# The first gate and up pair as seven-product units, and a new handover from keys and values to the units

## The chip, the cores and the metric

The kernel runs on one core of one Trainium2 chip. The metric is the device time of one execution in microseconds (us). The engines of a core work side by side, each through its own list of instructions in order: TensorE (PE in the profile, its weight loads PEld), VectorE (DVE), ScalarE (ACT), GpSimd (POOL) and SyncE (SP). SP and POOL here only start DMAs, each into a queue of its own. They meet through semaphores: an instruction at the head of its list waits until what it reads is written and what it overwrites has been read, and everything behind it on that engine waits too.

## What is computed

Two branches share one input of 2048 tokens by 1024 and are mixed by a sigmoid gate for each token.

```python
g = _sigmoid((x * gate_w).sum(-1, keepdims=True))
a = _A_ref(x, A_wqkv, A_w_phi, A_wo)          # linear attention, 32 heads of 32
b = _B_ref(x, B_w_gate, B_w_up, B_w_down)     # gelu(x @ w_gate) * (x @ w_up) @ w_down, 3584 hidden
return g * a + (1 - g) * b

# in _A_ref, per head: q, k, v from x @ wqkv
pq, pk = q @ w_phi, k @ w_phi
phi_q = concat(softmax(pq), softmax(-pq));  phi_k = concat(softmax(pk), softmax(-pk))
kv = phi_k.T @ v;  z = phi_k.sum(over tokens)
o = (phi_q @ kv) / (phi_q @ z + 1e-6);  a = o @ wo
```

## The kernel before

**Numbers and passes.** All matrices are float32. A factor is kept as two float32r tiles, a high part (a copy by ACT: `high`, or the first half of `split`) and a low part (the rest, a subtraction by DVE: `low`). A product of two factors is three matmuls per 128 rows of depth: `PASSES` is high by high, high by low, low by high.

**First and second keys-and-values pass.** The tokens are four blocks of 512 (`BLK`). The loop `for hh in range(2)` makes keys and values of 16 heads for all tokens, in 16 chunks of 128 tokens. A chunk is 48 matmuls (`keys_values`, L202): 24 into a PSUM bank of keys (`m` = 0), 24 into a bank of values (`m` = 1). `features` turns the keys into both softmaxes: on DVE a maximum, a minimum and two subtractions (L209 to L213), ACT takes the exponential, and then come the split of the values (`vs`), a sum, a reciprocal, a product and the split into `f`; `accumulate` (L235, 8 matmuls) adds the chunk to `kv` two chunks later. Four PSUM banks (`turn_bank`) hold keys and values and four (`bank`) hold the running `kv`. `meanwhile` names what DVE does beside a chunk: the split of a part of x for a later block (`load_x`), or the gate's logits for 128 tokens (`gate`, one DVE instruction over 1024 columns). In the second pass the split x of blocks 0 and 1 is made a second time, since the first pass overwrote it, and `query_weights` folds `w_phi` into the query weights (L136), for eight head groups, one half of the fold after each half of a chunk. Loads come through `stage`, three buffers of 512 KB filled by SP.

**Units.** Gate, up and query projections run as units: one unit takes two blocks of 512 tokens (a half) and two blocks of 128 weight columns, and makes the four results by seven products in place of eight (a Strassen scheme). A product is 12 matmuls (`product`, L768). A unit has seven slots; its products `c` ("z", operand 6) and "v" (operand 5) run in slots 2 and 4 of the next unit. The products need sums of the x blocks (`x_sums`: four DVE instructions for each quarter of the depth; split into `xs`, operands 1, 2, 4, 5) and sums of the weight blocks (x, y, z and v in `weights`). PE and DVE follow program order, in the units ACT and SP do so too. The order of DVE and ACT work within the units comes from a planner (`run_slot`) which keeps a clock for DVE and ACT, and due times in slots for each piece.

**The handover.** The first pair of gate and up columns for the first half isn't made by units: `project` (L103) makes it plainly, eight times 24 matmuls, between the keys and values and the first unit. Under these 192 matmuls DVE and ACT make the x sums of the first half, the last features, the split of z and the first unit's weights. The first half has 30 units then, the second 32.

**The turn.** When the second half begins, `second_half` (L535 and on) loads its operands in 14 parts through four buffers. After part n is split, SP loads part n + 4 into the buffer just read (`load`, L551). `late_sums` makes the second half's x sums earlier, beside the units of the first.

After the units, the down and output projections (L1203) follow; the change doesn't touch them.

Of the kernel before, what the change touches and what calls it, by code (L numbers as in the profile page):

```python
# [16 lines left out]
P = 128  # L17
KC = D // P
# [13 lines left out]
def tile_gated_mix(ctx: ExitStack, tc: tile.TileContext, x, xT, wkT, wqT, wv, w_phi, wo,  # L32
# [56 lines left out]

    def new_weight():  # L90
        return ring.tile([P, 2, KC, P], F32R, tag="wgu", name="wgu", bufs=2)
# [32 lines left out]
    xs_late = [dram.tile([P, KC // 2, BLK], F32, name=f"xs{k}") for k in range(4)]  # L124
# [16 lines left out]

    PE, DVE, ACT, SP = (getattr(mybir.EngineType, n) for n in ("PE", "DVE", "Activation", "SP"))
    with tc.tile_pool(name="kw", bufs=1) as kw, tc.tile_pool(name="kp", bufs=1) as kp, \
            tc.tile_pool(name="kl", bufs=1) as kl, tc.manual_schedule(engines={PE, DVE}):
        ones = kp.tile([P, P], F32, name="ones")
        nc.vector.memset(ones, 1.0)
        mask = kp.tile([P, 4, 32], F32, name="mask")
        nc.vector.memset(mask, 0.0)
        for j in range(4):
            nc.vector.memset(mask[32 * j:32 * j + 32, j, :], 1.0)  # L150
        ones_r = kp.tile([P, P], F32R, name="ones_r")
        nc.vector.tensor_copy(ones_r, ones)
        phi_c = kp.tile([P, NG, 32], F32, name="phi_c")

        warm = turn_bank()
        for _ in range(7):
            nc.tensor.matmul(warm[:, :P], ones, ones, start=True, stop=True)
        nc.scalar.dma_start(phi_c, w_phi.rearrange("(g h) d f -> (h d) g f", h=4))

        spare = []  # L160
        for tag, n in (("vs", 1), ("f", 2)):
            for _ in range(2):
                t = kp.tile([P, n, 1024], F32, tag=tag, name="early", bufs=2)
                spare += [t[:, i] for i in range(n)]
        for _ in range(2):
            t = ring.tile([P, 2, 1024], F32, tag="wgu", name="early", bufs=2)
            spare += [t[:, i] for i in range(2)]
        spare = [kp.tile([P, 1024], F32, tag="gw", name="early", bufs=1)] + spare
        zb = kl.tile([P, NG, 2, 32], F32, name="zb")

        def gate(c):
            s = stage((0, 1024, x[c * P:(c + 1) * P, :]))
            nc.vector.scalar_tensor_tensor(s, s, 1.0, gw, op0=OP.mult, op1=OP.mult,
                                           accum_out=logit[:, c:c + 1])

        def block_diagonal(hh):
            bd = kw.tile([P, 4, 4, 32], F32, name="bd")
            for j in range(4):
                nc.vector.tensor_tensor(bd[:, j], phi_c[:, 4 * hh + j:4 * hh + j + 1, :].to_broadcast([P, 4, 32]),
                                        mask, OP.mult)  # L180
            return bd

        def staged_pair(hh, kc, into=None):
            return stage((0, 512, wkT[hh, kc]), (512, 512, wv[hh, kc]), into=into)

        def fold(hh, kc, bd, s=None, pf=None):

            s = staged_pair(hh, kc) if s is None else s
            w = kw.tile([P, 2, 1024], F32R, tag="wkv", name="wkv", bufs=KC)
            pf = bank() if pf is None else pf  # L190
            for j in range(4):
                nc.tensor.matmul(pf[:, j * P:(j + 1) * P], s[:, j * P:(j + 1) * P],  # L192
                                 bd[:, j].rearrange("p a b -> p (a b)"), start=True, stop=True)
            with urgent():
                split(w[:, 0, 512:], w[:, 1, 512:], s[:, 512:])
                split(w[:, 0, :512], w[:, 1, :512], pf)
            return w

        def keys_values(ps, w, b, t, kc, parts=range(2)):
            for i, (a, e) in enumerate(PASSES):  # L200
                for m in parts:
                    nc.tensor.matmul(ps[m], xb[b, kc // 4][:, a, kc % 4, t * P:(t + 1) * P], w[:, e, m * 512:(m + 1) * 512],  # L202
                                     start=kc == 0 and i == 0, stop=kc == KC - 1 and i == 2)

        def features(ps, vs, f, zacc, first):

            pk = ps[0].rearrange("p (h f) -> p h f", f=32)
            mm = kp.tile([P, 2, 16], F32, tag="mm", name="mm", bufs=2)
            nc.vector.tensor_reduce(mm[:, 0, :], pk, AX.X, OP.max)  # L209
            nc.vector.tensor_reduce(mm[:, 1, :], pk, AX.X, OP.min)  # L210
            e = kp.tile([P, 2, 16, 32], F32, tag="e", name="e", bufs=2)
            nc.vector.tensor_tensor(e[:, 0], pk, mm[:, 0, :].unsqueeze(2).to_broadcast([P, 16, 32]), OP.subtract)
            nc.vector.tensor_tensor(e[:, 1], mm[:, 1, :].unsqueeze(2).to_broadcast([P, 16, 32]), pk, OP.subtract)  # L213
            nc.scalar.activation(e, e, AF.Exp)
            yield
            split(vs[:, :, 0], vs[:, :, 1], ps[1].rearrange("p (a b) -> p a b", b=64))
            yield
            r = kp.tile([P, 2, 16], F32, tag="r", name="r", bufs=2)
            nc.vector.tensor_reduce(r, e, AX.X, OP.add)
            nc.vector.reciprocal(r, r)  # L220
            yield
            nc.vector.tensor_tensor(e, e, r.unsqueeze(3).to_broadcast([P, 2, 16, 32]), OP.mult)
            yield
            split(f[:, 0], f[:, 1], e.rearrange("p s h f -> p s (h f)"))
            yield
            if first:
                nc.vector.tensor_copy(zacc, e)
            else:
                nc.vector.tensor_tensor(zacc, zacc, e, OP.add)

        def accumulate(pkv, vs, f, first, last):

            for d in range(8):
                heads = slice(64 * d, 64 * d + 64)
                nc.tensor.matmul(pkv[d // 2][:, d % 2], vs[:, d].rearrange("p a b -> p (a b)"), f[:, :, :, heads],  # L235
                                 start=first and d % 2 == 0, stop=last, skip_group_check=True)

        def finish_kv(hh, pkv):

            t = kp.tile([P, 4, 2, 2, 64], F32, tag="e", name="kv_t", bufs=2)  # L240
            for n, p in enumerate(pkv):
                nc.scalar.activation(t[:, n], p[:, :, 0], AF.Copy)
                nc.vector.tensor_tensor(t[:, n], p[:, :, 1], t[:, n], OP.add)
            low_rows = kp.tile([P, 4, 2, 2, 64], F32, tag="e", name="kv_l", bufs=2)
            nc.scalar.activation(low_rows[:64], t[64:], AF.Copy)
            nc.vector.tensor_tensor(t[:64], t[:64], low_rows[:64], OP.add)
            kv_c = kl.tile([P, 4, 2, 2, 32], F32, name="kv_c")
            for h in range(2):
                q = slice(32 * h, 32 * h + 32)
                nc.vector.transpose(kv_c[q].rearrange("p a b c d -> p (a b c) d"),  # L250
                                    t[q].rearrange("p a b c d -> p (a b c) d")[:, :, q])
            for s in range(2):
                nc.gpsimd.dma_start(kz[0][64 * s:64 * s + 64, 4 * hh:4 * hh + 4], kv_c[:64, :, :, s])

        def z_parts(zacc, zs):
            zs = zs.rearrange("p i (s a) b -> p i s (a b)", s=2)
            split(zs[:, 0], zs[:, 1], zacc.rearrange("p s h f -> p s (h f)"))
            return zs

        def finish_z(hh, zs, parts=range(2)):  # L260
            for s in parts:
                pz = bank() if hh else turn_bank()
                for i in range(2):
                    nc.tensor.matmul(pz, ones_r, zs[:, i, s], start=i == 0, stop=i == 1)
                z4 = pz.rearrange("p (g h f) -> p g h f", g=4, h=4)
                for h in range(4):
                    q = slice(64 * s + 32 * (h % 2), 64 * s + 32 * (h % 2) + 32)
                    nc.scalar.activation(zb[q, 4 * hh:4 * hh + 4, h // 2], z4[q, :, h, :], AF.Copy)

        gates = list(range(S // P))  # L270

        def meanwhile(hh, n, chunks):

            x_part = lambda b, j: lambda: load_x(b, (j,))
            done, part = divmod(n - 3, 4)
            if hh == 0 and n < 3:
                return [x_part(1, j) for j in ((0,), (1, 2), (3,))[n]]
            if done in (0, 1):
                return [x_part((chunks[4 * done][0] + 2) % 4, part)]
# [965 lines left out]
```

## Time and profile before

| | us |
|---|---|
| median of 3 runs (2365.52 to 2365.89) | 2365.73 |
| the profiled execution: its own time | 2365.71 |
| the profiled execution: span from first to last instruction | 2363.9 |
| PE busy | 2357.4 |
| DVE busy | 1800.6 |
| ACT busy | 1054.1 |

The span is 1.8 us shorter than the time of the same execution; this difference lies around the program. By the timeline the two keys-and-values passes end at 414.6 us from the start, the plain projections at 461.0, the units at 1674.1, and the rest is the two last projections. Spans of matmuls are modelled, so the distance from one matmul's start to the next one's tells more than the busy time: 12 matmuls of 512 columns take 2.72 us.

### The profile page before, as it was taken

To read this page: it belongs to the slowest core of one execution; us is meant where nothing else is said; L and a number is where in the kernel's file an instruction comes from. 1 tells how busy PE (TensorE), PEld (TensorE's weight loads), DVE (VectorE), ACT (ScalarE), POOL (GpSimd) and SP (SyncE) were. 2 spreads that over 40 slices of the span, in tenths; PEclk is the share of its full clock that TensorE was granted. 3 is DMA by queue.
4 is the path that set the end of the run, shared out by engine and by line. 5 is a ranking of instruction groups with operands and counts; after the bars stand their busy time and mean duration, and the time that the engine had idled before them with its cause. 6 is when DMAs were issued, how large, how long until landed. Compare 5 with 4: busy or idle time off the path is not lost.

```text
span 2363.9 us, 28280 instructions
## 1 busy us (share of the span) xinstructions
PE 2357.4 (100%) x10625; PEld 1958.3 (83%) x10625; DVE 1800.6 (76%) x2353; ACT 1054.1 (45%) x1380; POOL 159.2 (7%) x297
## 2 busy tenths in 40 slices
PE   9999999999999999999999999999999999999999
PEld 8888888888888888888888888888888888888887
DVE  7887878878798777767888877777574868867873
ACT  4324332546545544456565666665433323323221
POOL 0000000111111111110010000000000000000000
PEclk9999999999999999999999999999999999999999
DMA  5112233544454556474444444444784767977874
GB/s 177 49 45 89 83 117 116 198 165 167 152 181 168 185 195 209 175 268 140 143 153 144 149 140 149 139 139 134 242 304 159 275 228 246 339 267 274 286 268 137
DMA packets 152618, 425.11 MB, mean 180 GB/s; under 512 B 21408, under 2 KB 21408, under 8 KB 152480
## 3 DMA queue, kind: packets, MB, share of 16 engines
q1 hardware_dynamic: 123840, 329.30, 42.0%
q0 software_dynamic: 27600, 93.87, 10.4%
q8 instruction: 83, 1.36, 0.2%
q14 instruction: 55, 0.45, 0.1%
q10 hardware_dynamic: 1040, 0.13, 0.0%
HBM read 328.34 MB, written 94.90 MB: 179 GB/s over the span
## 4 chain that ended last, share of the span: by engine, by line
PE 99%; DMA 1%; DVE 0%; issue 0%; ACT 0%; SPq 0%; DVEq 0%
PE po L1203 29%; PE a L768 21%; PE pd L202 15%; PE c L768 14%; PE b L768 7%; PE p L768 7%; PE pg L235 1%; PE misc L980 1%; PE pd L103 1%; PE pg L103 1%; PE pd L136 1%; PE pd L192 0%; DMA early<-in_wkT 0%; DMA stage<-in_w_gate 0%; PE pg L192 0%; DMA phi_c<-in_w_phi 0%
## 5 line engine op out<-in xcount | busy, mean ns | idle before, releaser
L202 PE MATMUL pd<-wkv,x 128*128 128x512 f32 x1536 | 360.0, 391 | 0.0
L202 PEld LDWEIGHTS pd<-wkv,x 128*128 128x128 f32 x1536 | 284.8, 188 | 57.3 <-DVE x L44 0.3
L1203 PE MATMUL po<-tw,wgu 128*128 128x512 f32 x1344 | 309.8, 389 | 0.0
L1203 PEld LDWEIGHTS po<-tw,wgu 128*128 128x128 f32 x1344 | 252.3, 188 | 52.3
L414 ACT ACTIVATE wgu<-stage 128x1024 fp32r<-128x1024 f32 x147 | 155.4, 1057 | 236.6 <-DVE stage L1093 160.6
L417 DVE TENSOR_TENSOR wgu<-stage,wgu 128x1024 fp32r<-128x1024 f32 x147 | 179.2, 1219 | 78.8 <-ACT wgu L414 77.8
L417 DVE TENSOR_TENSOR tyz<-stage,tyz 128x1024 fp32r<-128x1024 f32 x126 | 153.4, 1217 | 51.7 <-ACT tyz L414 51.7
L768 PE MATMUL b<-s,tyz 128*128 128x512 f32 x744 | 179.0, 389 | 1.1 <-DVE s L417 1.1
L768 PE MATMUL a<-s,tyz 128*128 128x512 f32 x744 | 179.1, 389 | 0.0
L768 PE MATMUL p<-s,tyz 128*128 128x512 f32 x744 | 178.9, 389 | 0.0
L768 PE MATMUL a<-s,v 128*128 128x512 f32 x744 | 178.8, 389 | 0.0
L768 PE MATMUL c<-x,tyz 128*128 128x512 f32 x744 | 178.8, 389 | 0.0
L768 PE MATMUL c<-x,wgu 128*128 128x512 f32 x744 | 178.8, 389 | 0.0
L768 PE MATMUL a<-x,wgu 128*128 128x512 f32 x744 | 178.7, 389 | 0.0
L768 PEld LDWEIGHTS b<-s,tyz 128*128 128x128 f32 x744 | 139.6, 188 | 30.5 <-DVE s L417 1.6
L768 PEld LDWEIGHTS a<-s,tyz 128*128 128x128 f32 x744 | 139.5, 188 | 29.5 <-DVE tyz L417 0.4
L768 PEld LDWEIGHTS c<-x,tyz 128*128 128x128 f32 x744 | 139.7, 188 | 29.3
L768 PEld LDWEIGHTS c<-x,wgu 128*128 128x128 f32 x744 | 139.7, 188 | 29.2
L768 PEld LDWEIGHTS p<-s,tyz 128*128 128x128 f32 x744 | 139.6, 188 | 29.0
L768 PEld LDWEIGHTS a<-s,v 128*128 128x128 f32 x744 | 139.6, 188 | 29.0
L768 PEld LDWEIGHTS a<-x,wgu 128*128 128x128 f32 x744 | 139.6, 188 | 29.0
L1203 PE MATMUL po<-tw,wl 128*128 128x512 f32 x672 | 157.2, 389 | 0.0
(186 smaller groups left out, 3506.7 us busy)
## 6 DMA issues: line engine op xcount, KB each, us to landing
stage<-lm SPq DMA_DIRECT2D x98, 512.0 KB, 4.7
sr<-in_w_down SPq DMA_DIRECT2D x84, 512.0 KB, 5.4
sl<-lm SPq DMA_DIRECT2D x70, 512.0 KB, 4.6
lm<-h POOLq DMA_DIRECT2D x112, 256.0 KB, 2.3
stage<-in_w_gate SPq DMA_DIRECT2D x43, 512.0 KB, 3.8
stage<-in_w_up SPq DMA_DIRECT2D x43, 512.0 KB, 3.7
stage<-la SPq DMA_DIRECT2D x28, 512.0 KB, 5.4
tg<-stage POOLq DMA_DIRECT2D x26, 512.0 KB, 3.0
```

Source lines behind the costliest of these rows:

```text
L103: nc.tensor.matmul(pg, w[:, a, kc, :], xb[b, kc // 4][:, e, kc % 4, :], start=kc == 0 and i == 0, stop=kc == KC - 1 and i == 2)
L136: nc.tensor.matmul(pf[:, j * P:(j + 1) * P], s[:, (4 * k + j) * P:(4 * k + j + 1) * P], bp.rearrange("p a b -> p (a b)"), start=True, stop ...
L202: nc.tensor.matmul(ps[m], xb[b, kc // 4][:, a, kc % 4, t * P:(t + 1) * P], w[:, e, m * 512:(m + 1) * 512], start=kc == 0 and i == 0, stop= ...
L235: nc.tensor.matmul(pkv[d // 2][:, d % 2], vs[:, d].rearrange("p a b -> p (a b)"), f[:, :, :, heads], start=first and d % 2 == 0, stop=last ...
L414: nc.scalar.activation(dst, src, AF.Copy)
L417: nc.vector.tensor_tensor(dst, src, dst_h.bitcast(F32), OP.subtract)
L768: nc.tensor.matmul(dst, w[:, h, 4 * part + kc, :], xq[:, e, kc, :], start=first and kc == 0 and i == 0, stop=kc == 3 and i == 2, skip_grou ...
L980: nc.tensor.matmul(po[p], kbs[:, p].rearrange("p a b -> p (a b)"), pts[:, q, p, :], start=q == 0, stop=q == 1)
L1203: nc.tensor.matmul(ps[c], lefts[s][:, a, m, c * P:(c + 1) * P], made[k][:, e, m], start=d == 0 and m == 0 and n == 0, stop=d == n_duo - 1 ...
```

## The change

The first half gets all 32 units: the first gate and up pair goes through units too, and the 192 plain matmuls go. So the x sums of the first half, the first unit's weights and the second unit's raw weights must be ready when the keys and values end.

- **First pass.** `store_x` writes the split x of blocks 0 and 1 to DRAM (`x_parts`, four DMAs of 2 MB on SP, at chunks 3, 5, 7 and 9). Eight of the gate's logits move here, one at each of chunks 3 to 10, beside the x part.
- **Second pass.** `reload_x` reads the split x back (four DMAs of 2 MB on SP) in place of eight loads and splits. `early_sums` makes the x sums of the first half (chunks 4, 5, 7, 8) and POOL writes them to DRAM (`x_sum`). Both halves of a query fold follow the chunk; four groups are folded there (chunks 1 to 4), the other four in the handover. The first unit's weights are made at chunks 9 and 11; the z sum of the first heads moves from chunk 1 to chunk 6.
- **`features`** adds to `zacc` before the low part of `f`, not after it. The split of the values stands by itself (`split_values`).
- **Chunks 14 and 15** of the second pass are woven: keys of 14, keys of 15, values of 14, values of 15.
- **Handover.** Between the last values and the first unit PE has four folds and two `accumulate`; ACT and DVE follow an order written by hand. The pools are closed and opened so that new tiles may wait for single tiles (`reuse_waits="tile"`).
- **Turn.** `second_half` loads part n + 3 after part n, into the buffer that part n - 1 has left.

```diff
+    def store_x(b, k):
+        nc.sync.dma_start(x_parts[b][k], xb[b, k].bitcast(F32))
+    def reload_x(b, k):
+        xb[b, k] = new_quarter(b, k)
+        nc.sync.dma_start(xb[b, k].bitcast(F32), x_parts[b][k])
...
+    def quarter_sums(e, o):
+        nc.vector.tensor_tensor(o[:, BLK:], o[:, BLK:], o[:, :BLK], OP.subtract)
+        nc.vector.tensor_tensor(o[:, :BLK], e[:, :BLK], o[:, :BLK], OP.subtract)
...
+        es = e.rearrange("p s h f -> p s (h f)")
+        nc.scalar.activation(f[:, 0], es, AF.Copy)
         if first:
             nc.vector.tensor_copy(zacc, e)
         else:
             nc.vector.tensor_tensor(zacc, zacc, e, OP.add)
+        yield
+        nc.vector.tensor_tensor(f[:, 1], es, f[:, 0].bitcast(F32), OP.subtract)
...
+    def early_sums(kc):
+        r1, r2 = (stage() for _ in range(2))
+        x_load(0, kc, r1, r2)
+        x_sums(0, kc, r1, r2)
...
+            if hh == 0:
+                works.append(x_part(done + 2, part))
+                if part % 2 == 0:
+                    store_x(done, part // 2)
+            elif part % 2 == 0:
+                reload_x(done, part // 2)
+        if n in GATES[hh]:
+            works.append(lambda c=gates.pop(0): gate(c))
+        if hh and n in SUMS:
+            works += [lambda: None] * (not works) + [lambda: early_sums(SUMS.index(n))]
+    SUMS = (4, 5, 7, 8)
+    GATES = (range(3, 14), (1, 2, 3, 6, 10))
...
+            elif hh and n == 14:
+                ps, later = ([turn_bank(), turn_bank()] for _ in range(2))
+                for kc in range(KC):
+                    keys_values(ps, wkv[kc], b, t, kc, (0,))
+                pending.pop(0)()
+                for kc in range(KC):
+                    keys_values(later, wkv[kc], *chunks[15], kc, (0,))
+                for kc in range(KC):
+                    keys_values(ps, wkv[kc], b, t, kc, (1,))
+                pending.pop(0)()
+            elif hh and n == 15:
+                ps = later
+                for kc in range(KC):
+                    keys_values(ps, wkv[kc], b, t, kc, (1,))
...
-        first_g = {0: project(first_w[0], 0, turn_bank())}
...
-        gs = [project(second_w, j) for j in range(2)]
...
+        folds = [fold_in(last_q[0], turn_bank)]
+        zs = slot().rearrange("p i (s a) b -> p i s (a b)", s=2)
+        split_values(ps, vs)
+        rest(folds[0])
+        for accumulate_last in pending:
+            accumulate_last()
+        folds.append(fold_in(last_q[1], turn_bank))
+        for i in range(2):
+            for do in early[i]: do()
+        raw_sum(2)
+        kv = finish_kv(1, pkv)
+        next(kv)
+        rest(folds[1])
+        high(zs[:, 0], z_rows)
+        rest(kv)
+        folds.append(fold_in(last_q[2], turn_bank))
+        rest(folds[2])
+        first_z = slot()
+        high(flat(first_z)[0], even_w)
+        low(flat(first_z)[1], even_w, flat(first_z)[0])
+        folds.append(fold_in(last_q[3], bank))
+        rest(folds[3])
+        for i in range(2, 4):
+            for do in early[i]: do()
+        raw_sum(3)
+        low(zs[:, 1], z_rows, zs[:, 0])
...
-                if n + 4 < len(parts):
-                    load(n + 4)
+                if 0 < n < len(parts) - 3:
+                    load(n + 3)
...
-            mine = [(half, k, m) for m in range(1 - half, NF // 2) for k in "gu"]
+            mine = [(half, k, m) for m in range(NF // 2) for k in "gu"]
...
+        late, early = (psum_b.enter_context(tc.tile_pool(name=n, bufs=1, space=PSUM, reuse_waits="tile"))
+                       for n in ("pl", "pe"))
...
+        clock[:] = 5.5, 4.2
```

`fold_in` issues the two halves of a fold (16 matmul instructions, into two banks); `fold_out`, run by `rest`, copies both banks by ACT and stores them by POOL. `early[i]` is the high and the low part of one half of `xs[0]` (i = 0, 1) or of `xs[1]` (i = 2, 3). The last line sets the planner's start clocks of DVE and ACT for the first unit.

More of the change, by code (lines that the diff above doesn't have):

```diff
@@ new lines, in tile_gated_mix @@
+    for _ in range(7):
+        nc.tensor.matmul(warm[:, :P], ones, ones, start=True, stop=True)
+    nc.scalar.dma_start(phi_c, w_phi.rearrange("(g h) d f -> (h d) g f", h=4))
+    spare = []
+    for tag, n in (("vs", 1), ("f", 2)):
+        for _ in range(2):
+            t = kp.tile([P, n, 1024], F32, tag=tag, name="early", bufs=2)
+            spare += [t[:, i] for i in range(n)]
+    for _ in range(2):
+        t = ring.tile([P, 2, 1024], F32, tag="wgu", name="early", bufs=2)
+        spare += [t[:, i] for i in range(2)]
@@ new lines, in staged_pair, with fold @@
+    def staged_pair(hh, kc, into=None):
+        return stage((0, 512, wkT[hh, kc]), (512, 512, wv[hh, kc]), into=into)
+    def fold(hh, kc, bd, s=None, pf=None):
+        s = staged_pair(hh, kc) if s is None else s
+        w = kw.tile([P, 2, 1024], F32R, tag="wkv", name="wkv", bufs=KC)
+        pf = bank() if pf is None else pf
+        for j in range(4):
+            nc.tensor.matmul(pf[:, j * P:(j + 1) * P], s[:, j * P:(j + 1) * P],
+                             bd[:, j].rearrange("p a b -> p (a b)"), start=True, stop=True)
+        with urgent():
+            split(w[:, 0, 512:], w[:, 1, 512:], s[:, 512:])
+            split(w[:, 0, :512], w[:, 1, :512], pf)
+        return w
@@ new lines, in accumulate, with finish_kv @@
+    def accumulate(pkv, vs, f, first, last):
+        for d in range(8):
+            heads = slice(64 * d, 64 * d + 64)
+            nc.tensor.matmul(pkv[d // 2][:, d % 2], vs[:, d].rearrange("p a b -> p (a b)"), f[:, :, :, heads],
+                             start=first and d % 2 == 0, stop=last, skip_group_check=True)
+    def finish_kv(hh, pkv):
+        t = kp.tile([P, 4, 2, 2, 64], F32, tag="e", name="kv_t", bufs=2)
+        for n, p in enumerate(pkv):
+            nc.scalar.activation(t[:, n], p[:, :, 0], AF.Copy)
+            nc.vector.tensor_tensor(t[:, n], p[:, :, 1], t[:, n], OP.add)
+        yield
+        low_rows = kp.tile([P, 4, 2, 2, 64], F32, tag="e", name="kv_l", bufs=2)
+        nc.scalar.activation(low_rows[:64], t[64:], AF.Copy)
+        nc.vector.tensor_tensor(t[:64], t[:64], low_rows[:64], OP.add)
+        kv_c = kl.tile([P, 4, 2, 2, 32], F32, name="kv_c")
+        for h in range(2):
+            q = slice(32 * h, 32 * h + 32)
+            nc.vector.transpose(kv_c[q].rearrange("p a b c d -> p (a b c) d"),
+                                t[q].rearrange("p a b c d -> p (a b c) d")[:, :, q])
+        for s in range(2):
+            nc.gpsimd.dma_start(kz[0][64 * s:64 * s + 64, 4 * hh:4 * hh + 4], kv_c[:64, :, :, s])
@@ new lines, in tile_gated_mix @@
+                if turn:
+                    wkv = fresh
+                if len(pending) > 1:
+                    pending.pop(0)()
+                if hh and n == 0:
+                    zs = z_parts(zacc, new_weight())
+                if hh == 0 and n == 14:
+                    bd = block_diagonal(1)
+            if n == 0:
+                zacc = kp.tile([P, 2, 16, 32], F32, name="zacc")
+                pkv = []
+            vs = kp.tile([P, 8, 2, 64], F32R, tag="vs", name="vs", bufs=2)
@@ new lines, in tile_gated_mix @@
+            f = kp.tile([P, 2, 2, 512], F32R, tag="f", name="f", bufs=2)
+            steps = features(ps, f, zacc, n == 0)
+            next(steps)
+            works = meanwhile(hh, n, chunks)
+            for work in works[:1]:
+                work()
+            if hh and n == 15:
+                split_values(*waiting)
+            if hh and n == 14:
+                waiting = ps, vs
+            elif not (hh and n == 15):
+                split_values(ps, vs)
+            if not (hh == 0 and n == 14):
+                for _ in steps:
+                    pass
@@ new lines, in tile_gated_mix, with values @@
+            for work in works[1:]:
+                work()
+            def values(hh=hh, pkv=pkv, vs=vs, f=f, n=n):
+                if n == 0:
+                    pkv += [bank((P, 2, 2, 2, 64)) for _ in range(4)]
+                accumulate(pkv, vs, f, n == 0, n == 15)
+                if n == 15 and hh == 0:
+                    for _ in finish_kv(hh, pkv):
+                        pass
+            pending.append(values)
+            if hh and n == 9:
+                odd_w, even_w = stage((0, 1024, wq_fold[1])), stage((0, 1024, wq_fold[0]))
+                first_x, first_y = new_weight(), new_weight()
+                pair = lambda w: [w[:, i].rearrange("p a b -> p (a b)") for i in range(2)]
+                split(*pair(first_x), even_w)
@@ L410, in slot @@
+    halves = ExitStack()
+    mid = ctx.enter_context(tc.tile_pool(name="mid", bufs=1, side="right", reuse_waits="tile"))
+    xa = halves.enter_context(tc.tile_pool(name="xa", bufs=1, side="right", reuse_waits="tile"))
+    homes = xa.tile([P, 2, 1024], F32, tag="pts", name="wq", bufs=1)
+    last_q += [(EARLY_Q + 2 + i, stage((0, 1024, wqT[EARLY_Q + 2 + i]), into=homes[:, i]), bps[2 + i]) for i in range(2)]
     def slot():
@@ L659, in drain @@
                     fillers.pop(0)[1]()
-        raws = [mid.tile([P, 2, 2 * BLK], F32, tag="tyz", name="raw", bufs=3) for _ in range(3)]
-        raws.append(fa.tile([P, 2, 2 * BLK], F32, tag="pts", name="raw", bufs=1))
-        for kc, r in enumerate(raws):
-            if kc == 3:
-                staged_up = stage((0, 1024, w_up[1]))
-            x_load(0, kc, r[:, 0], r[:, 1])
-        sums = {}
-        def highs(*which):
-            for k, kc in which:
-                high(xs[k][:, 0, kc, :], sums[kc][k])
@@ L693, in tile_gated_mix @@
-        for kc in range(3):
-            add(kc)
-        up_w = new_weight()
-        high(flat(up_w)[0], staged_up)
-        low(flat(up_w)[1], staged_up, flat(up_w)[0])
-        us = [project(up_w, j) for j in range(2)]
-        highs((2, 0), (3, 0))
-        for j in range(2):
-            multiply(gelu(first_g[j]), first_u[j], j, 0)
-        lows((1, 0))
-        add(3)
-        hs = [gelu(gs[0])]
-        start(weights(0, *units[0]))
-        now[0] = -20
-        lows((2, 0), (3, 0))
-        drain(-4)
```

580 lines of the change are left out of this document (274 added, 306 removed).

## The prediction

> **What bounds the kernel now.** I read the page first, then the windows by stage, the waits of PE, and the chain of waits around the places that the change touches.
>
> ```profile
> span 2363.9 us, 28280 instructions
> PE 2357.4 (100%) x10625; PEld 1958.3 (83%) x10625; DVE 1800.6 (76%) x2353; ACT 1054.1 (45%) x1380; POOL 159.2 (7%) x297
> PE 99%; DMA 1%; DVE 0%; issue 0%; ACT 0%; SPq 0%; DVEq 0%
> ```
>
> The chain that ended last is 99% PE. So work on other engines is worth nothing unless PE waits for it, and there are two ways to gain: fewer matmuls, or the few places where PE does wait. The windows show where these are (columns: length, then busy time and count for PE, PEld, DVE, ACT, POOL, then granted clock, DMA share and GB/s).
>
> ```profile
> 4.00:8.00 4.00, 3.77 (x20) 3.08 (x19) 2.27 (x7) 2.57 (x5) 0.00 (x0) 1.00 1.02 364
> 26.00:400.00 374.00, 373.96 (x1851) 316.95 (x1850) 296.01 (x380) 125.95 (x158) 5.85 (x10) 1.00 0.25 80
> 400.00:461.00 61.00, 61.00 (x285) 51.10 (x284) 54.12 (x79) 29.93 (x48) 4.70 (x8) 1.00 0.58 193
> 461.00:1040.00 579.00, 579.00 (x2553) 478.94 (x2553) 452.00 (x662) 298.51 (x418) 81.99 (x152) 1.00 0.52 182
> 1040.00:1060.00 20.00, 18.85 (x84) 15.29 (x83) 15.82 (x18) 11.19 (x14) 2.16 (x4) 1.00 0.88 278
> ```
>
> PE is full through both keys-and-values passes, the handover (400 to 461) and the units, save one hole at 1040 to 1060, the turn. The handover of the kernel before costs no wait at all, so the change can't win one there; it can only lose one.
>
> **The matmuls that go.** The chain, in order of time, around the handover:
>
> ```profile
> 413.63 0.95 PE pg L235 x8
> 414.58 5.47 PE pd L103 x24
> 421.00 10.91 PE pd L103 x48
> 432.86 5.47 PE pd L103 x24
> 439.24 21.76 PE pg L103 x96
> 461.00 2.72 PE a L768 x12
> ```
>
> The 192 plain matmuls are the four L103 pieces (24 + 48 + 24 + 96). Two more units are 2 x 7 products of 12, 168 matmuls. So 24 matmuls go, and one is 2.72 / 12 = 0.227 us: **5.4 us less**. That is the whole algebraic gain, 0.23% of the time.
>
> **The folds.** Each half of a fold (L136) now sits alone between other matmuls:
>
> ```profile
> 257.70 5.63 PE L202 MATMUL pd<-wkv,x 128*128 128x512 f32 x24
> 263.17 1.05 PE L136 MATMUL pd<-bp,stage 128*128 128x128 f32 x8
> 263.98 5.70 PE L202 MATMUL pd<-wkv,x 128*128 128x512 f32 x24
> ```
>
> The 24 matmuls that follow a fold take 0.07 us longer than those before it. Before there are 16 such changes; after, the two halves stand together (four in the second pass), and the four groups of the handover make two runs: six. Ten times 0.08 is **0.8 us less**; the bounds are 0 and 16 x 0.08 = 1.3. The four folds of the handover are the same instructions as before, so they cost nothing new.
>
> **The turn.** SP's rows, then ACT's, DVE's and PE's:
>
> ```profile
> 1038.11 3.89 SPq L551 DMA_DIRECT2D raw<-in_xT  x2
> 1042.05 0.97 SPq L51 DMA_DIRECT2D stage<-in_w_gate  x2
> 1048.38 1.06 ACT L414 ACTIVATE wgu<-stage 128x1024 fp32r<-128x1024 f32 x1 [3.72 <-DMA stage<-in_w_gate]
> 1055.10 0.39 PE L768 MATMUL b<-s,tyz 128*128 128x512 f32 x1
> 1055.36 2.35 DVE L417 TENSOR_TENSOR s<-x,s 128x1024 fp32r<-128x1024 f32 x2
> 1056.63 2.79 PE L768 MATMUL b<-s,tyz 128*128 128x512 f32 x11 [1.15 <-DVE s L417]
> ```
>
> The second refill of a buffer (up to 1042.0) waits on SP until DVE has read that buffer, and the gate weight's load stands behind it in SP's list. It lands late, ACT waits 3.72 us, everything behind on ACT and DVE shifts, and PE loses 1056.63 - 1055.10 - 0.23 = 1.3 us. With the refill one part later into a buffer left one part earlier, SP needs only the release behind the refill at 1038.1, so the weight load can go some 3 us earlier, more than twice the hole: **1.3 us less**. What is late next is the operand refills, now three parts ahead. The parts stand about 3.9 us apart (the two refills from 1038.1 to 1042.0 show such a step), so three are over 11 us. The bounds are 0 gained (another load is late) and 1.3; I take 1.3, since the release that SP waited for is exactly what moves.
>
> **The handover.** Count from the last matmul of the values of chunk 15. PE then has a fold (1.7 us: 16 instructions at 0.81 / 8 from the fold rows above), two `accumulate` (0.95 each), three folds (5.1): 8.7 us, and then the first product of unit 0, which needs a PSUM bank that the folds used. ACT and DVE have to follow (rows of the second pass, columns: busy, mean ns):
>
> ```profile
> L219 DVE TENSOR_REDUCE r<-e 128x32 f32<-128x1024 f32 x16 | 19.3, 1208 | 0.6 <-ACT e L214 0.6
> L139 ACT ACTIVATE stage<-pd 128x512 f32<-128x512 f32 x16 | 9.5, 595 | 14.1 <-PE pd L136 13.9
> L43 ACT ACTIVATE x<-stage 128x1024 fp32r<-128x1024 f32 x8 | 8.5, 1057 | 8.5 <-DMA stage<-in_xT 8.4
> L243 DVE TENSOR_TENSOR kv_t<-pg,kv_t 128x256 f32<-128x256 f32 x4 | 1.4, 416 | 2.7 <-ACT kv_t L242 2.7
> L250 DVE STREAM_TRANSPOSE kv_c<-kv_t 32x512 f32<-32x512 f32 x2 | 1.4, 701 | 0.0
> L246 DVE TENSOR_TENSOR kv_t<-kv_t,kv_l 64x1024 f32<-64x1024 f32 x1 | 1.2, 1218 | 1.1 <-ACT kv_l L245 1.1
> L242 ACT ACTIVATE kv_t<-pg 128x256 f32<-128x256 f32 x4 | 1.2, 391 | 0.0
> ```
>
> ACT in its written order: values high 0.6, two fold copies 1.2, two highs of `xs[0]` 2.1, four copies of kv 1.2, two fold copies 1.2, z high 1.06, the copy kv_l 1.06, two fold copies 1.2. The first fold's second bank is ready at 1.7, so its copy ends at 2.3; the 7.8 us behind it follow with nothing between, and the third fold's second copy ends at 10.1. If unit 0's first product starts in that bank, PE waits 10.1 - 8.7 = **1.4 us**. The lower bound is 0 (its bank was one of the second fold's). The upper is a pool change that waits for the last fold's copies: ACT goes on with the high of z's weights (1.06) and two copies (1.2) to 12.4, a wait of 3.7. In between: kv_t's buffer may be that of the first fold's raw weights, which POOL still stores:
>
> ```profile
> wq<-stage POOLq DMA_DIRECT2D x8, 512.0 KB, 2.9
> stage<-in_wqT SPq DMA_DIRECT2D x8, 512.0 KB, 3.6
> ```
>
> The first fold's copies end at 2.3, the store at 5.2, and kv's copies could start at 4.4: another 0.8. The last two folds' weights load (3.6 us) into space that the last keys and values just left; the first of them is needed at 3.6 + 1.7 = 5.3, so it is in time by over a microsecond. I take 1.4, the walk through rows as they stand.
>
> Behind that, DVE: values low 0.7 (to 1.5), two lows of `xs[0]` (1.2 each, to 5.7), kv adds (to 7.1), after kv_l at 8.9 the add and the transposes 2.6 (to 11.5), z weights' low (12.7), lows of `xs[1]`, the second behind ACT's highs (12.4 + 2.1 = 14.5) at 15.7. Unit 0's third product, which reads `xs[1]`, starts at 10.1 + 2.7 + 0.2 + 2.7 = 15.7 and needs that second half 1.4 us later. It holds, with 1.4 us to spare.
>
> **The two passes.** The second pass has room: 9.6 us of x sums (16 DVE instructions of about 0.6) and five logits come in, eight x lows (1.2 each) and thirteen logits go, and DVE is busy 296 of 374 us. In the first pass eight logits come in, 1.3 us each with the read of the sum. For each chunk the new place of `zacc` covers a wait that DVE has now, 1.13 us in the row below, so the pace stays. What it can lose is the distance to PE:
>
> ```profile
> 66.37 0.68 DVE L213 TENSOR_TENSOR e<-mm,pd 128x512 f32<-128x512 f32 x1
> 66.96 1.22 DVE L44 TENSOR_TENSOR x<-stage,x 128x1024 fp32r<-128x1024 f32 x1
> 71.43 10.91 PE pd L202 x48
> 77.12 0.68 DVE L213 TENSOR_TENSOR e<-mm,pd 128x512 f32<-128x512 f32 x1
> 83.43 1.23 DVE L44 TENSOR_TENSOR f<-e,f 128x1024 fp32r<-128x1024 f32 x1 [1.13 <-ACT f L43]
> 87.50 0.67 DVE L213 TENSOR_TENSOR e<-mm,pd 128x512 f32<-128x512 f32 x1
> 45.09 11.89 SPq L51 DMA_DIRECT2D stage<-in_xT  x3
> ```
>
> Chunk 3's keys are read by 67.05, and chunk 5 writes a bank again at 71.43: 4.4 us of room. The 2 MB stores are SP's, not DVE's, but the x low at 66.96 now overwrites what a store reads. The loads for these chunks go out 10 to 20 us ahead (45.09 to 57), and a store that needs no buffer goes with them. So I cost the stores, reloads and sums at nothing; if that cover goes, see the last rival.
>
> **Sum.** 2363.9 - 5.4 - 0.8 - 1.3 + 1.4 = 2357.8 us of span; with 1.8 us around it, 2359.6. The profiled execution (2365.71) stands at the median of 2365.73, so no correction: **2359.6 us**, 6.1 below. Between 2361.0 and 2370.5, within 0.2%, a measurement of this kernel can't tell it from no change.
>
> **Rivals.** *The handover gives it back* (0.24). ACT's copies stand in one line with no hole, so every bank or buffer that changes hands later than I think adds its whole delay: 3.7 for the pool change in place of 1.4, and 0.8 more for kv_t's buffer, so 4.5 us of wait, 3.1 over the forecast. That is 2362.7, and 2361 to 2363 with a part of it or a half microsecond elsewhere, no measurable change. For it speaks that the plain projections were 43 us of cover and are now 8.7; against it, that each piece found a place in the walk. The windows show a granted clock of 1.00 everywhere, also where PE waits 1.3 us. The Trainium skill, page "TensorE: Matmul & The Clock Gate", section "HAM oscillation", warns of PE gaps over about 3.4 us, after which the clock halves for a window of that length; by it a gap of 4.5 would cost an estimated 1.7 more. No trace here has a gap that long, so neither shows.
>
> *The turn stays* (0.10). Some other refill is late and 1.3 is not won: 2360.9. With the handover as forecast that is just still faster; with a fifth of a microsecond more it isn't.
>
> *Slower: the stores hold up the first pass* (0.06). If SP issues a store only at its place (chunk 3, about 67), the x low behind it waits for 2.1 MB to leave: between 5.8 us (at the 364 GB/s of the fastest window) and 4 x 2.9 = 11.6 us (four stores of 512 KB). DVE's distance is 4.4, so PE loses 1.4 to 7.2, and at the three later stores, with the distance used up and 2 x 1.5 us won back between stores (DVE's pace from 77.12 to 87.50 is 10.4, PE's is 10.91 + 0.95), 3 to 9 each: 2359.6 + 10 to 34, 2370 to 2394. It decides from a store landing later than about 71. Against it stands the SP row above. [...]
>
> **Chances and range.** Forecast 0.60 (2357 to 2361), handover 0.24, turn 0.10, slower 0.06. Faster by over 0.2%: 0.60 and half of the turn's, 0.65; same 0.29; slower 0.06. The floor is 2365.7 - 5.4 - 1.3 - 1.3 = 2357.7 with no wait at all and all of the folds' changes, and some tenths for small waits elsewhere: low 2357.2. The high end takes in the handover rival: 2363.6.
>
> **What would show it.** 10601 matmuls on PE. No L103 row, 64 x 12 in each L768 group. Around the handover the chain should show the folds in two runs and then a wait of about 1.4 us of unit 0's first product for ACT's fold copy; a wait for `xs[1]`, `first_z` or z would show my DVE walk wrong. At the turn no wait of PE for `s`. In the first pass no wait of PE for DVE or ACT; one there would show the last rival. PE's waits together over 4 us would make the forecast wrong.

## The result, and the profile after

| | us |
|---|---|
| before, median of 4 runs (2365.52 to 2365.89) | 2365.68 |
| after, median of 4 runs (2397.43 to 2398.33) | 2397.81 |
| after / before, 95% interval | 1.0136 [1.0118, 1.0153] |
| span of the profiled execution, before | 2363.9 |
| span of the profiled execution, after (its time 2398.33) | 2396.5 |

The forecast was 2359.6 us. The kernel became 32 us slower, and by none of the ways that the prediction named. The page of the changed kernel, with the same three lines as before:

```profile
span 2396.5 us, 28304 instructions
PE 2390.1 (100%) x10601; PEld 1954.6 (82%) x10601; DVE 1806.0 (75%) x2354; ACT 1053.9 (44%) x1378; POOL 170.9 (7%) x318
PE 99%; DMA 1%; DVE 0%; issue 0%; ACT 0%; SPq 0%; ACTq 0%; DVEq 0%
```

PE issues 10601 matmuls, the 24 fewer that were forecast, and is busy 32.7 us longer with them. The windows by stage (columns as in the prediction) and all of PE's waits in the changed kernel:

```profile
26.00:400.00 374.00, 374.00 (x1789) 309.53 (x1788) 311.15 (x407) 113.81 (x142) 14.05 (x25) 1.00 0.43 143
461.00:1040.00 579.00, 579.00 (x2508) 470.97 (x2507) 455.61 (x663) 301.06 (x420) 81.62 (x151) 1.00 0.51 179
1040.00:1060.00 20.00, 20.00 (x89) 16.27 (x88) 13.97 (x15) 12.80 (x18) 1.08 (x2) 1.00 0.72 242
```

```profile
PE pd L192 <- DVE ones L181: 1.1, 1, 1.1
PE po L1310 <- DVE wgu L512: 0.7, 1, 0.7
PE pg L225 <- DMA early<-in_wkT: 0.7, 2, 0.5
PE pg L225 <- DVE bd L212: 0.2, 1, 0.2
```

Nothing is missing in these windows: PE is full in each, the clock is 1.00, and the waits add up to 2.7 us. But in the 579 us from 461 on PE gets through 2508 matmuls, where it did 2553 before. The loss sits inside the matmuls. The chain shows it in the plainest place, the keys and values of one chunk, which the change doesn't touch in this pass:

```profile
48.64 11.19 PE pd L235 x48
59.83 0.96 PE pg L271 x8
60.79 11.19 PE pd L235 x48
```

Before, these 48 matmuls took 10.91 us (L202 in the prediction's fence of the passes): 227 ns from one start to the next, now 233. The groups by line (busy, mean ns of one) show the same for some operand pairs and not for others. Before:

```profile
L1203 PE MATMUL po<-tw,wgu 128*128 128x512 f32 x1344 | 309.8, 389 | 0.0
L1203 PE MATMUL po<-tyz,wgu 128*128 128x512 f32 x672 | 155.2, 389 | 0.0
L768 PE MATMUL c<-x,tyz 128*128 128x512 f32 x744 | 178.8, 389 | 0.0
L980 PE MATMUL misc<-pts,kbs 128*128 128x512 f32 x128 | 35.2, 396 | 0.0
```

After:

```profile
L235 PE MATMUL pd<-wkv,x 128*128 128x512 f32 x1536 | 366.7, 396 | 0.0
L1310 PE MATMUL po<-tw,wgu 128*128 128x512 f32 x1344 | 310.1, 389 | 0.0
L854 PE MATMUL c<-x,tyz 128*128 128x512 f32 x768 | 190.0, 396 | 0.0
L854 PE MATMUL a<-s,v 128*128 128x512 f32 x768 | 189.5, 395 | 0.0
L854 PE MATMUL a<-x,wgu 128*128 128x512 f32 x756 | 182.5, 390 | 0.0
L1310 PE MATMUL po<-tyz,wgu 128*128 128x512 f32 x672 | 160.2, 396 | 0.7 <-DVE wgu L512 0.7
```

The last projections are code that the change left alone. Of two of their groups with the same stationary name, `po<-tw,wgu` keeps its 389 ns and `po<-tyz,wgu` goes to 396. A name in the second place is the stationary operand, in the first the moving one. So it isn't the clock, the stage or the shape; it is something about the pair of tiles. The fourth row of before shows that one group had the longer time already.

The time by stage, from the starts of matmuls in the traces (first and second pass begin with their first `pd<-wkv,x`, the units end with the start of their last matmul; the last column is experiment e1, below):

| us | before | after | e1 |
|---|---|---|---|
| up to the first keys | 7.5 | 7.7 | 7.4 |
| first pass | 201.9 | 205.8 | 201.8 |
| second pass and handover | 251.5 | 211.5 | 206.9 |
| units (5339 matmuls before, 5511 after and in e1) | 1213.1 | 1273.3 | 1249.8 |
| last projections | 690.1 | 698.2 | 690.5 |
| span | 2363.9 | 2396.5 | 2356.3 |

### The profile page after: what moved, and what is told of

It is laid out like the page before. It is cut to its first block, busy times and chain, and to the rows that moved or that the text cites. A ratio compares the mean times of both kernels' runs of the same rounds, so it can differ in the third digit from the quotient of the medians.

```text
span 2396.5 us, 28304 instructions
## 1 busy us (share of the span) xinstructions
PE 2390.1 (100%) x10601; PEld 1954.6 (82%) x10601; DVE 1806.0 (75%) x2354; ACT 1053.9 (44%) x1378; POOL 170.9 (7%) x318
## 4 chain that ended last, share of the span: by engine, by line
PE 99%; DMA 1%; DVE 0%; issue 0%; ACT 0%; SPq 0%; ACTq 0%; DVEq 0%
PE po L1310 29%; PE a L854 22%; PE c L854 15%; PE pd L235 15%; PE b L854 7%; PE p L854 7%; PE pg L271 1%; PE misc L1085 1%; PE pd L144 0%; PE pd L225 0%; DMA early<-in_wkT 0%; PE pd L545 0%; PE pg L225 0%; DMA sr<-in_w_down 0%; DMA phi_c<-in_w_phi 0%; PE pg L545 0%
## 5 line engine op out<-in xcount | busy, mean ns | idle before, releaser
L235 PE MATMUL pd<-wkv,x 128*128 128x512 f32 x1536 | 366.7, 396 | 0.0
L854 PE MATMUL c<-x,tyz 128*128 128x512 f32 x768 | 190.0, 396 | 0.0
L854 PE MATMUL a<-s,v 128*128 128x512 f32 x768 | 189.5, 395 | 0.0
L854 PE MATMUL b<-s,tyz 128*128 128x512 f32 x756 | 187.1, 396 | 0.0
L854 PE MATMUL a<-s,tyz 128*128 128x512 f32 x768 | 185.5, 390 | 0.0
L854 PE MATMUL p<-s,tyz 128*128 128x512 f32 x756 | 184.7, 393 | 0.0
L854 PE MATMUL c<-x,wgu 128*128 128x512 f32 x756 | 183.6, 391 | 0.0
L854 PEld LDWEIGHTS c<-x,tyz 128*128 128x128 f32 x768 | 144.5, 188 | 34.2
L854 PEld LDWEIGHTS a<-s,v 128*128 128x128 f32 x768 | 144.5, 188 | 34.0
L1310 PE MATMUL po<-tyz,wgu 128*128 128x512 f32 x672 | 160.2, 396 | 0.7 <-DVE wgu L512 0.7
```

What stands on the lines that cost most here:

```text
L854: nc.tensor.matmul(dst, w[:, h, 4 * part + kc, :], xq[:, e, kc, :], start=first and kc == 0 and i == 0, stop=kc == 3 and i == 2, skip_grou ...
L1310: nc.tensor.matmul(ps[c], lefts[s][:, a, m, c * P:(c + 1) * P], made[k][:, e, m], start=d == 0 and m == 0 and n == 0, stop=d == n_duo - 1 ...
```

## The experiments

**The suspect.** The change moves three pools of SBUF to its other end. The diff has these lines, which "the change" above didn't show:

```diff
-    with tc.tile_pool(name="kw", bufs=1) as kw, tc.tile_pool(name="kp", bufs=1) as kp, \
+    kw = weights_kv.enter_context(tc.tile_pool(name="kw", bufs=1, side="right"))
-    mid = ctx.enter_context(tc.tile_pool(name="mid", bufs=1))
+    mid = ctx.enter_context(tc.tile_pool(name="mid", bufs=1, side="right", reuse_waits="tile"))
-    with tc.tile_pool(name="xa", bufs=1) as xa, tc.tile_pool(name="fa", bufs=1) as fa, \
+    xa = halves.enter_context(tc.tile_pool(name="xa", bufs=1, side="right", reuse_waits="tile"))
```

A pool on the right is laid from the last free byte of a partition downward, and by the program's allocation that byte is 229344, which isn't a multiple of 64. So all tiles of `kw`, `mid` and `xa` start 96 bytes further, modulo 256, than those of the pools on the left. Before, the two operands of every matmul of 512 columns started alike, save one pair (`kbs` against `pts`, 128 bytes apart: the L980 row). **Theory: a matmul takes about 7 ns longer when its moving and its stationary operand start at different places modulo some power of two.** Adding up, over all matmuls of 512 columns, the distance between starts above 226.7 ns gives 2.6 us before and 41.1 after; 2396.5 - 38.5 = 2358.0 us would be left of the span. Rivals: each operand's own address counts (a boundary of 64 bytes); or the placement has nothing to do with it, and the new DMAs or pool rules slow PE.

**e1, e2: the right edge.** One unused tile at the right edge moves the three pools, with nothing else changed: 24 floats make the starts agree modulo 256, 8 floats leave them 64 apart.

```diff
+    edge = ctx.enter_context(tc.tile_pool(name="edge", bufs=1, side="right"))
+    edge.tile([P, 24], F32, name="edge")
     kw = weights_kv.enter_context(tc.tile_pool(name="kw", bufs=1, side="right"))
```

> The changed kernel with 96 unused bytes at the right-hand edge of SBUF, so that the right-hand pools (kw, then mid and xa) start at a multiple of 128 bytes and not 32 past one; nothing else changes. Start-address theory (a matmul whose moving and stationary operands differ in address by 32 modulo 64 takes 233 ns in place of 227): every 512-column matmul goes back to 227 ns, the sum of the excess falls from 41.1 to about 2.6 us, and the time from 2397.8 to about 2359.3. Traffic theory (the 8 MB of x stored and the 8 MB read back, and the sums in DRAM, slow PE's reads): unchanged, 2397 to 2398, since the traffic is the same. Place theory (the right-hand half of SBUF is slower as such): unchanged.

> As the one with 96 unused bytes, but with 32, so that the right-hand pools start 64 past a multiple of 128. Start-address theory with a unit of 64 bytes: as with 96, about 2359.3 and 227 ns. With a unit of 128 bytes: the slow pitch stays, about 2397.

e1: **2358.49 us** (median of 7), ratio to before on the same chip (2365.01 us) 0.9971 [0.9960, 0.9982]. e2: 2394.72 us (one run). The groups of e1 and then of e2:

```profile
L237 PE MATMUL pd<-wkv,x 128*128 128x512 f32 x1536 | 357.8, 390 | 0.0
L856 PE MATMUL c<-x,tyz 128*128 128x512 f32 x768 | 184.5, 389 | 0.0
L1312 PE MATMUL po<-tyz,wgu 128*128 128x512 f32 x672 | 155.6, 389 | 0.5 <-DVE wgu L514 0.5
```

```profile
L856 PE MATMUL c<-x,tyz 128*128 128x512 f32 x768 | 189.4, 394 | 0.0
L1312 PE MATMUL po<-tyz,wgu 128*128 128x512 f32 x672 | 157.3, 392 | 0.9 <-DVE wgu L514 0.7
```

96 bytes of unused memory take back 39 us, and the changed kernel is then faster than the one before. The instructions, DMAs and pool rules are those of the change, so none of these was the cause. A boundary of 64 bytes isn't the condition either.

**e3, e4: the kernel before, moved.** An unused tile of 32 bytes behind the pool `ring` puts everything but `ring` 32 bytes on (e3); the same tile ahead of `ring` moves all (e4).

```diff
     ring = ctx.enter_context(tc.tile_pool(name="ring", bufs=2))
+    edge = ctx.enter_context(tc.tile_pool(name="edge", bufs=1))
+    edge.tile([P, 8], F32, name="edge")
```

> The kernel before, with 32 unused bytes between the pool ring and all later pools: ring stays at a multiple of 64, kw, kp, mid, xa, fa, fp and op start 32 past one. No work changes. If it is the difference between the two operands that counts: slow are keys and values (1536), the products of plain x with z (744) and two kinds of the last stage (1344 and 672), 4296 x 6.7 ns = 29 us, about 2395; the products of sums with y, z and v stay at 227. If every operand off a multiple of 64 costs: also those (2976) and the rest of the last stage (1008), in all 8280 x 6.7 = 55 us, about 2421. If addresses don't count: 2365.7.

> The kernel before, with 32 unused bytes ahead of ring too, so that every operand of every large matmul starts 32 past a multiple of 64. If the difference between the operands counts: 2365.7, 227 ns throughout. If every operand off a multiple of 64 costs: over 9900 matmuls x 6.7 ns = 66 us, about 2432.

e3: 2400.69 us. e4: 2364.55 us (one run each; before on the same chip 2365.01). (e3 is 6 above what the theory gave. In its trace the 4460 matmuls of the units whose own operands agree take 228.8 ns from start to start on average, 9.3 us over 226.7 in sum; the theory had counted them at nothing, and e8 shows why they are slower.) The chain of e3, then that of e4, at the same chunk:

```profile
48.06 11.20 PE pd L204 x48
```

```profile
47.62 10.91 PE pd L204 x48
```

The slowdown can be put into the old kernel with 32 bytes, and it goes when the other operands are moved along. So neither operand's own address decides (in e4 none is a multiple of 64); the difference does.

**e5: 128 or 256.** The changed kernel with 56 floats at the edge in place of 24.

> The changed kernel with 224 bytes left free at the right edge of SBUF in place of 96: the right pools then start 128 bytes (modulo 256) away from the left ones, and every tile is a multiple of 128 bytes from every other. If the pitch needs start addresses that agree modulo 128, this runs as e1 did: 226.7 ns a matmul, about 2358.5 us. If they must agree modulo 256 (the attention matmuls of the kernel before, 128 apart, took 234.2), it is slow again: 231 to 238 ns a matmul, 2394 to 2400 us.

2394.05 us (median of 2), ratio 1.0123 [1.0105, 1.0142]; 48 matmuls of keys and values:

```profile
48.31 11.16 PE pd L237 x48
```

Agreement modulo 128 isn't enough.

**e8: the cost by itself.**

```diff
+    def group(name, movs, wts, n=32):
+        t = psum.tile([P, BLK], F32, tag="t", name=name, bufs=4)
+        for i in range(n):
+            m, w = movs[i % len(movs)] // 4, wts[i % len(wts)] // 4 + P * i
+            nc.tensor.matmul(t, wt[:, w:w + P], mov[:, m:m + BLK], start=i == 0, stop=i == n - 1)
+    for d in (0, 4, 16, 32, 64, 96, 128, 160, 192, 224, 256, 288, 320, 384, 448, 512):
+        group(f"w{d}b", (0,), (d,))
```

> The disputed cost by itself. Nothing of the reference is computed: 40 groups of 32 matmuls (128x128 by 128x512, float32r) read two tiles whose first bytes agree modulo 512; the start of the stationary operand (w), of the moving one (m), or of both is put off by the bytes in the group's name, and in the alt groups only in every second matmul. If the difference modulo 256 sets the pitch: w0, w256, w512, m256 and both at about 226.7 ns a matmul, all other w and m groups at 231 to 238. If modulo 128: w128, w384 and m128 at 226.7 too. If each operand's own address counts: both32 and both64 slow as well. In the altw groups (every second weight off) half of the matmuls should be slow: a mean of about 230.

(With the warm-up there are 38 groups, in one run.) In the alt groups every second matmul has the stationary operand put off, or the moving one, or both; in the last kind each matmul has one of the two put off, in turn. Some of the groups, busy time of 32 matmuls and mean ns of one:

```profile
L50 PE MATMUL w96b<-mov,wt 128*128 128x512 f32 x32 | 7.7, 396 | 0.0
L50 PE MATMUL m32b<-mov,wt 128*128 128x512 f32 x32 | 7.6, 395 | 0.0
L50 PE MATMUL w128b<-mov,wt 128*128 128x512 f32 x32 | 7.6, 394 | 0.0
L50 PE MATMUL w4b<-mov,wt 128*128 128x512 f32 x32 | 7.6, 394 | 0.0
L50 PE MATMUL w192b<-mov,wt 128*128 128x512 f32 x32 | 7.5, 392 | 0.0
L50 PE MATMUL both32b<-mov,wt 128*128 128x512 f32 x32 | 7.5, 390 | 0.0
L50 PE MATMUL w512b<-mov,wt 128*128 128x512 f32 x32 | 7.4, 390 | 0.0
L50 PE MATMUL w256b<-mov,wt 128*128 128x512 f32 x32 | 7.4, 389 | 0.0
L50 PE MATMUL w0b<-mov,wt 128*128 128x512 f32 x32 | 7.4, 389 | 0.0
```

The distance from start to start tells more than the busy time. Its mean in each group, in ns, from the trace (first and last matmul of a group left out):

| stationary put off by | ns | | moving or both put off | ns |
|---|---|---|---|---|
| 0, 256, 512 | 226.7, 226.7, 227.1 | | moving by 256 | 227.4 |
| 4, 16, 32 | 232.3, 233.3, 233.1 | | moving by 32, 128 | 233.3, 232.7 |
| 64, 96, 128 | 233.4, 234.2, 232.3 | | moving by 64 | 229.0 |
| 160, 224, 288 | 233.2, 233.2, 233.2 | | both by 32, 64, 128 | 227.4, 227.4, 228.1 |
| 320, 384 | 233.2, 232.4 | | every 2nd stationary by 32, 64, 128 | 234.4, 230.2, 233.4 |
| 192, 448 | 229.1, 228.9 | | every 2nd moving by 32, 64, 128 | 231.8, 231.5, 230.1 |
| 0, the last group of all | 227.8 | | the two in turn by 32, 64, 128 | 230.6, 231.6, 230.0 |
| | | | every 2nd pair by 32, 64, 128 | 231.6, 231.8, 228.3 |

Where all pairs of a group are alike, the difference modulo 256 sets the pitch, from 4 bytes on; a moving operand 64 bytes ahead is the cheapest of the unequal ones (some 2.3 ns more in place of 5.6 to 7.5). Where pairs alternate, the difference of a matmul's own pair isn't all that counts. With every second stationary operand off, the expected 230 ns, half of the matmuls slow, came out for 64 bytes alone; by 32 and 128 nearly every step is slow. And where each pair agrees in itself but not with its neighbour (last row), it is slower too: the neighbour's operands count as well as a matmul's own.

The steps one by one show more. The groups with equal starts whose mean is above 226.7 all follow a group at other addresses: their first 4 to 10 steps are uneven (in the last group 234, 229, 231, 231, 236, 228, 232, 231), and those behind them are at 226.7. Only the stationary operand put off by 256 shows no such stretch. The changed kernel has the same: the products `p<-s,tyz` (both operands on the right, alike) that come after `a<-x,wgu` (both on the left, alike) take 236, 233, 236, 224, 231, 236, 228, 233 and 231 ns for their first nine steps, on average of 62 products, and then 226.6. So a change of addresses from one group to the next can cost some steps even where every pair agrees, here nine of a product's 12.

**e6, e7: the turn.** The kernel before with the new order of refills alone (e6), and e1 with the old order (e7):

```diff
-                if n + 4 < len(parts):
-                    load(n + 4)
+                if 0 < n < len(parts) - 3:
+                    load(n + 3)
```

> The kernel before with the turn's refill order of the change alone (part n + 3 after part n, from n = 1). By the forecast PE's wait for s at the turn (1.3 us, at 1055 to 1057) is gone and the time is 2364.4. If another load is late in its place, the wait is there with another name and the time stays at 2365.7. Nothing else moves: L768 and L1203 keep 226.7 ns.

> The changed kernel with the 96 free bytes of e1 and the turn's old order (part n + 4 after part n). If the order of the refills is what removed the wait at the turn, 1.3 us come back (span 2357.6 against 2356.3 of e1). If the other edits removed it (the first unit in place of plain products changes when SP and DVE are free), it stays away: span 2356.3.

e6: 2364.0 us against 2364.78 for the kernel before on the same chip, ratio 0.9996 [0.9988, 1.0005], which the times can't tell from nothing. The waits of PE in e6 can, and the units take 1211.7 us in its trace where they took 1213.1 in the trace of before:

```profile
PE pg L192 <- DMA early<-in_wkT: 1.1, 1, 1.1
PE pd L157 <- DVE ones L146: 1.1, 1, 1.1
```

Both are at the start of the program. The wait for `s` is gone. e7: 2358.6 us, span 2356.8, and its waits:

```profile
PE pg L227 <- DMA early<-in_wkT: 1.4, 1, 1.4
PE pd L194 <- DVE ones L183: 1.1, 1, 1.1
PE po L1312 <- DVE wgu L514: 0.7, 1, 0.7
PE po L1312 <- ACT wgu L511: 0.4, 1, 0.4
```

No wait at the turn here either. So in these traces the order of refills is enough to remove the wait from the kernel before, and not needed in the changed one. Which other edit does it there wasn't tried.

## Why the prediction was wrong

**The step that failed** is in "The matmuls that go": "24 matmuls go, and one is 2.72 / 12 = 0.227 us". The price was read from the kernel before and held for all 10601 that stay. Behind it stands the sentence "there are two ways to gain: fewer matmuls, or the few places where PE does wait". There is a third quantity, what one matmul takes, and it changed: 41.1 us above 226.7 ns a matmul after, 2.6 before (units 23.1, keys and values 9.6, last projections 7.4, attention 0.9, the rest 0.1). The first pass, whose stores the prediction costs "at nothing", lost 3.9 us to the pitch (201.9 to 205.8, and 201.8 in e1). No rival priced this. The slower rival, a store that holds up the first pass, had nothing to do with it: SP issued the four stores of 2 MB from 26.0 to 54.5 us, ahead of their places, they landed 8.8 to 13.3 us later, so all before the 71 us from which the rival counted a loss, and PE has no wait in that pass after its start.

Without that cost, e1 stands for what was forecast: 2358.49 us, inside the range. That it comes within 1.1 us of 2359.6 is in part luck: two terms of the sum weren't there, with opposite signs, and a gain that no term held came in. With e1 the rest of the sum can be read term by term.

- **24 matmuls, -5.4**: right. 10601 matmuls, those of 512 columns at 226.7 ns in e1 but for 0.9 us in sum.
- **The turn, -1.3**: right for the profiled execution, and the edit named for it is enough by itself (e6), but not the only one that does it (e7). The size isn't firm: with the same old order the hole is 0.8 us in e3's trace and 0.5 in e4's, and the medians of e6 and of before on its chip are 0.8 apart.
- **The folds, -0.8**: mis-sized. The extra 0.07 us (0.08 in the sum) was read from busy times, whose ends are modelled and overlap the next instruction. The chain counts from start to start. Before, then e1:

```profile
277.88 5.46 PE pd L202 x24
285.18 5.47 PE pd L202 x24
269.68 0.89 PE pd L136 x8
```

```profile
262.08 10.91 PE pd L237 x48
272.99 1.78 PE pd L144 x16
```

  A chunk with its two half folds took 5.46 + 5.47 + 2 x 0.89 = 12.71 us and takes 10.91 + 1.78 = 12.69 now: 0.02 for each of the eight groups, 0.2 us at most.
- **The handover, +1.4**: it isn't there. The chain of e1 runs through it without a hole, and ACT's rows stand beside it:

```profile
408.91 1.92 PE pg L273 x16
410.82 3.57 PE pd L547 x32
414.40 1.79 PE pg L547 x16
416.18 2.89 PE a L856 x12
```

```profile
411.33 1.20 ACT L280 ACTIVATE kv_t<-pg 128x256 f32<-128x256 f32 x4
412.39 1.12 ACT L511 ACTIVATE wq<-pd 128x512 f32<-128x512 f32 x2
413.34 1.10 ACT L511 ACTIVATE tyz<-zacc 128x1024 fp32r<-128x1024 f32 x1
414.47 1.05 ACT L284 ACTIVATE kv_l<-kv_t 64x1024 f32<-64x1024 f32 x1
415.44 1.06 ACT L511 ACTIVATE wq<-pd 128x512 f32<-128x512 f32 x2
```

  Two copies of a fold take 1.06 to 1.12 us back to back, not 1.2, and each instruction starts some 0.1 before the end of the one ahead, so the third fold's copies end at 416.50, 9.4 us after the first fold's start (407.12 in the chain) and not 10.1. PE's own walk took longer than the 8.7 us of the sum: 416.18 - 407.12 = 9.06, since a fold takes 1.78 to 1.79 us and not 1.7. And by the program's allocation unit 0's first product takes the bank of the third fold's *first* copy, free at 415.44 + 0.6 = 416.0, as the product starts. A delay of 0.17 us is left (2.89 for 2.72). The buffer of `kv_t` and the pool change held nothing up.
- **Not in the sum**: in e1 the attention matmuls (`misc<-pts,kbs`) go from 396 to 389 ns, since `kbs` and `pts` happen to agree there: 128 x 7.5 ns, the difference of the distance from start to start, is 1.0 us less. This is luck of the placement. Against it a new wait of 0.5 for `wgu` at the start of the last projections (690.5 us for 690.1). From the spans, 2363.9 - 2356.3 = 7.6, and 5.4 + 1.3 + 1.0 + 0.2 - 0.4 = 7.5.

**What was right and told nothing.** Every point of "what would show it" that could be seen came out as the forecast wanted (10601 matmuls, no wait at the turn, none in the first pass, waits together 2.7 us, below the 4 that were to refute it), save the wait at the handover, and yet the time was 38 us off. The list had no line for the pitch of a matmul. The sign was in the profile of before: one group of the same shape, in the same kernel, at 396 ns beside 389.

## What to carry to other kernels

Where PE is full, its time is a count times a price, and both need a forecast: when a change moves tiles, work out (for matmuls like these, the only kind tried here) where the moving and the stationary operand of each group start, modulo 256 bytes, in the allocation of both kernels. If a kernel whose PE is full becomes slower with no new wait, compare the start-to-start time of one unchanged group before anything else. A pool laid from the far edge takes its alignment from the edge, so pad it.

## What the runs showed of the hardware

- A float32r matmul of 128x128 by 128x512 starts 226.7 ns after the one before it when the operands' start addresses agree modulo 256, and 229 to 234 when they don't (e8, offsets of 4 to 512 bytes), at full clock (1.00) and with weight loads of 188 ns (median) in both cases. Across this kernel that is 2358.5 against 2397.8 us.
- It is the difference that counts. All operands 32 bytes off a 64-byte boundary cost nothing (e4, 2364.55 us).
- A matmul whose own operands agree is slowed by its neighbours: pairs that alternate between two offsets 32 bytes apart take 231.6 ns, and in six of seven equal groups that follow a group at other addresses the first 4 to 10 steps are uneven before they rest at 226.7 (e8).
- Why 256, why 64 bytes ahead costs less than the rest, and why it takes some steps to settle, no run here shows.
